# Pooled attention and a gated convolution FFN: v's first pooling addition by the loading DMA, ffn_in of sequence 0 by channel blocks, and a new order

## The chip, the cores and the metric

The kernel runs on one core of one Trainium2 chip. The metric is the device time in microseconds (us). TensorE (PE) multiplies matrices into PSUM; PEld is its weight load. VectorE (DVE), ScalarE (ACT) and GpSimd (POOL) work elementwise; SyncE (SP) issues DMAs only. All DMAs run on the same 16 DMA engines. Each engine works through its own instructions in program order and waits on semaphores for the others.

## The reference, cut to what matters

```python
def _attn_ref(q, k, v):                      # 8 sequences, 8 heads, 576 x 64, fp32
    k_p = k.reshape(B, H, Sp, 8, D).mean(axis=3)       # Sp = 72
    v_p = v.reshape(B, H, Sp, 8, D).mean(axis=3)
    scores = np.matmul(q, k_p.transpose(0, 1, 3, 2)) / np.sqrt(D)
    attn = softmax(scores)
    return np.matmul(attn, v_p)

def _moe_ref(x, w_in, conv_w, w_out):        # x: 8 x 576 x 512, d_ff = 1024
    h = np.maximum(x @ w_in, 0.0)
    conv_out = ...                           # depthwise, 3 taps along the sequence
    gate = 1.0 / (1.0 + np.exp(-conv_out))
    return h * gate @ w_out
```

The inputs and the output are fp32; inside, the kernel works in bf16 with fp32 sums.

## The kernel before

The eight sequences stand in four groups of two (groups 0 to 3). For each sequence the kernel loads q, k and v with a cast to bf16 (POOL's queue), pools and turns k, turns q, pools v, and then works through tiles of 128 rows: scores, maximum, shift, exponential, turning of e, product with v, division, turning of x. Then comes the FFN of the sequence: ffn_in, ReLU, the convolution with its sigmoid (a tanh), the gate, ffn_out and the store.

v's pooling is a tree of additions on VectorE. `load_v` (L280) brings a sequence with its eight neighbours side by side in 512 elements of a partition, in two DMAs of together 576 rows. `prep_v` (L459) adds the upper half to the lower three times (256, 128 and 64 elements wide, L464) and spreads the result over masked columns (L468). The ring of v has three buffers, so the load of sequence b waits until sequence b-3 is pooled.

`ffn_in` (L702) takes a block of 128 channels over half a sequence: four matmuls of 288 columns, and a ReLU for each block (`ffn_relu`, L713). Sequence 0 alone uses `ffn_in_tile` (L721) instead, a row tile of 128 (the last 64) against all eight channel blocks, with a ReLU for each tile (L736); it can begin with any one tile of x.

The convolution of a block runs either on TensorE with diagonal matrices (`ffn_conv`, L851) or, for the half sequences in `TAPS`, as three taps on ScalarE and VectorE (`ffn_tap`, L830, on a 576-wide view; L835, L837, L842). In group 2 and group 3, e and x are turned by DMAs on SP's queue (`att_send` L641, `att_out` L682), and in group 3 q as well (`q_send`, L505, one DMA transpose for a sequence). Outputs go through `osb`, a ring of five buffers, and are stored from SP's queue, in the last group from ScalarE's too.

Nothing is decided at run time. `Graph.ORDER` is a written-out list that a planner made: it names the operations in the order in which they are emitted, and an odd entry takes the second of two allowed engines (for a copy out of PSUM, VectorE first, ScalarE second). So it fixes the order on every engine and queue, POOL's loads and SP's transposes included. `FORMS` picks the TensorE tiling of some operations and `PLACES` the buffers and PSUM banks. The costs and the times of landing in `add(...)` served the planner alone and are not read at run time. A -1 in `ORDER` is a matmul on zeros (`fill`, L376) that keeps TensorE running while the first loads come in.

Of the kernel before, what the change touches and what calls it, by code (L numbers as in the profile page):

```python
# [33 lines left out]
class Graph:  # L34
# [25 lines left out]
    TAPS = ((4, 1), (5, 0), (5, 1), (6, 0), (6, 1), (7, 0))  # L60
    V_POOL = ()
    K_POOL = ()
    SHIFT_DVE = 1
# [3 lines left out]
        8, 26, 6, 2, -1, 18, 24, -1, 4, -1, -1, 36, -1, -1, 14, 38, -1, 10, 16, -1,  # L67
        -1, 34, 20, 22, 28, -1, 12, -1, -1, -1, 32, 30, 40, 92, 56, 94, 98, 96, 58, 104,
        101, 108, 103, -1, 106, 64, -1, 110, 42, 282, 48, 302, 284, 116, 50, 304, 112, 286, 114, 306,
        288, 118, -1, 308, 322, 324, 342, 310, 290, 120, 60, 313, 326, 328, -1, 344, -1, 362, 122, 346,  # L70
        364, 330, 348, 124, 366, 126, 333, 184, 293, 186, 334, 368, 62, 191, 294, 336, 189, 314, 68, 296,
        350, 52, 196, 353, 316, 192, 199, 354, 194, 370, 338, 356, 373, 504, 484, 74, 341, 506, 374, 486,
        0, 508, 318, 376, 510, 488, 358, 321, 524, 360, 216, 490, 526, 220, 218, 528, 378, 530, 222, 512,
        444, 380, 464, 394, 446, 66, 466, 448, 396, 514, 450, 54, 468, 400, 470, 128, 70, 298, 406, 301,
        44, 402, 398, 130, 382, 404, 132, 134, 472, 384, 46, 388, 386, 408, 475, 390, 410, 200, 532, 392,
        516, 492, 534, 434, 518, 495, 536, 202, 436, 438, 476, 538, 428, 478, 496, 430, 204, 228, 432, 498,
        231, 418, 440, 420, 412, 422, 442, 452, 416, 206, 414, 480, 72, 454, 224, 213, 424, 215, -1, 211,
        88, 209, 227, 252, 76, 426, 716, 483, 916, 255, 718, 544, 918, 520, 500, 720, 552, 503, 920, 523,
        696, 554, 136, 922, 698, 722, 456, 546, 557, 458, 540, 700, 876, 549, 248, 543, 878, 896, 560, 702,
        138, 251, 880, 704, 898, 724, 707, 460, 936, 140, 463, 562, 900, 727, 938, 582, 565, 142, 656, 584,  # L80
        902, 940, 80, 576, 882, 144, 594, 942, 578, 658, 586, 596, 580, 146, 708, 660, 598, 944, 884, 710,
        947, 624, 887, 148, 728, 150, 628, 588, 730, 626, 86, 712, 590, 715, 232, 948, 592, 924, 84, 904,
        736, 950, 78, 907, 606, 927, 738, 732, 888, 735, 608, 740, 612, 610, 890, 928, 742, 614, 930, 908,
        616, 744, 910, 952, 747, 630, 234, 748, 634, 954, 236, 632, 618, 750, 662, 932, 912, 620, 935, 152,
        752, 238, 622, 914, 754, 892, 243, 82, 646, 245, 894, 247, 636, 988, 241, 648, 1084, 990, 650, 1086,
        994, 992, 1100, 1088, 996, 1102, 600, 998, 1000, 154, 1116, 1104, 602, 1002, 1118, 604, 1030, 1106, 1120, 664,
        1032, 1004, 156, 568, 158, 1034, 160, 1122, 90, 676, 640, 1090, 638, 570, 642, 1092, 644, 678, 1006, 573,
        162, 558, 1012, 667, 680, 1008, 1014, 164, 1010, 652, 280, 1024, 1016, 668, 682, 1026, 670, 256, 1028, 260,
        566, 258, 1042, 263, 654, 1018, 1108, 1044, 1068, 1020, 1046, 1070, 772, 1022, 166, 672, 1072, 1052, 675, 168,
        1132, 684, 1054, 278, 1134, 774, 1056, 1136, 1058, 777, 264, 1138, 1322, 780, 1060, 1324, 1062, 1094, 687, 782,  # L90
        1124, 1096, 688, 1326, 785, 788, 550, 690, 1036, 266, 1306, 756, 1040, 268, 1328, 1308, 692, 1038, 790, 1064,
        695, 1110, 1074, 826, 1112, 793, 1076, 758, 1310, 820, 761, 1066, 828, 1126, 1098, 830, 832, 1128, 1312, 822,
        814, 1048, 824, 834, 1130, 816, 836, 860, 170, 818, 1140, 1050, 1338, 802, 862, 864, 808, 1330, 1340, 804,
        1342, 810, 806, 786, 1078, 172, 812, 274, 174, 270, 1080, 277, 1142, 1114, 273, 796, 1144, 850, 1082, 176,
        1570, 798, 854, 1572, 1146, 852, 838, 178, 800, 1574, 1332, 778, 840, 1344, 1334, 844, 842, 180, 1346, 1538,
        1230, 848, 1540, 846, 1232, 1542, 574, 866, 1234, 856, 1290, 1314, 1224, 868, 870, 1292, 1218, 1226, 872, 1220,
        1228, 1212, 1222, 1316, 1294, 1214, 1318, 1296, 1188, 1348, 1216, 874, 1298, 1190, 1544, 1238, 764, 1350, 1336, 1248,
        1206, 766, 858, 1192, 1546, 1240, 1300, 1208, 1250, 1164, 1320, 1210, 1302, 1576, 1554, 1506, 1252, 1304, 1166, 1264,
        1556, 769, 1200, 1254, 1508, 1352, 980, 1169, 1558, 1256, 1202, 794, 1510, 1194, 1560, 1242, 1410, 1204, 1578, 1196,
        182, 1412, 1258, 1422, 1414, 1562, 1266, 982, 1198, 1244, 1522, 1236, 1794, 1424, 1524, 1246, 1796, 1172, 1426, 1526,  # L100
        1512, 1548, 1798, 1174, 985, 1528, 1550, 1274, 1177, 1268, 1552, 1746, 1428, 1276, 1748, 1278, 1416, 1170, 1750, 1430,
        1564, 1260, 1432, 1580, 762, 1270, 1566, 1418, 1262, 1582, 1280, 770, 1752, 1272, 1420, 1398, 1282, 1530, 1436, 1404,
        1284, 1386, 1496, 972, 1568, 1286, 1472, 1406, 1388, 986, 1408, 1474, 974, 1498, 1514, 1392, 977, 1288, 956, 1488,
        964, 1390, 1476, 1394, 1490, 1532, 1396, 1400, 1534, 966, 1402, 1500, 1536, 1478, 1516, 1434, 1778, 1502, 1518, 1762,
        958, 1480, 1764, 1520, 1148, 1454, 1780, 1800, 1492, 1378, 1584, 969, 1482, 1150, 1494, 1802, 1766, 961, 1380, 1484,
        1768, 1626, 1178, 1153, 1456, 1644, 1462, 1628, 1782, 1154, 1646, 1458, 1630, 1638, 1648, 1464, 1804, 970, 1460, 1156,
        1806, 1383, 1640, 978, 1486, 1466, 1632, 1438, 1180, 1504, 1770, 1642, 1634, 1446, 1662, 1754, 1182, 1784, 1448, 1636,
        1664, 1440, 1468, 1808, 1656, 1674, 1772, 1185, 1450, 1158, 1666, 962, 1774, 1702, 1668, 1442, 1658, 1161, 1786, 1756,
        1704, 1444, 1670, 1452, 1758, 1362, 1660, 1706, 1370, 1760, 1672, 1470, 1708, 1650, 1372, 1776, 1694, 1686, 1788, 1652,
        1384, 1696, 1364, 1654, 1790, 1375, 1610, 1676, 1678, 1698, 1792, 1854, 1367, 1688, 1612, 1700, 1162, 1690, 1848, 1728,  # L110
        1586, 1680, 1692, 1376, 1856, 1730, 1615, 1842, 1712, 1682, 1368, 1602, 1858, 1732, 1850, 1684, 1186, 1714, 1860, 1734,
        1604, 1736, 1716, 1616, 1844, 1720, 1738, 1862, 1852, 1588, 1722, 1864, 1740, 1618, 1846, 1607, 1724, 1890, 1884, 1718,
        1608, 1872, 1710, 1726, 1886, 1742, 1594, 1894, 1620, 1744, 1591, 1596, 1910, 1592, 1888, 1874, 1599, 1878, 1896, 1918,
        1866, 1912, 1880, 1876, 1868, 1882, 1898, 1810, 1870, 1914, 1818, 1900, 1892, 1920, 1916, 1834, 1902, 1922, 1934, 1904,
        1924, 1820, 1938, 1906, 1936, 1812, 1908, 1928, 1623, 1926, 1624, 1354, 1932, 1930, 1826, 1600, 1823, 1940, 1836, 1825,
        1828, 1942, 1356, 1814, 1968, 1358, 1817, 1960, 1360, 1838, 1831, 1952, 1841, 1832, 1944, 1970, 1946, 1973, 1954, 1975,
        1948, 1962, 1957, 1951, 1976, 1958, 1964, 1967, 1978, 1984, 1982, 1981, 1986, 1990, 1989,
    )
    FORMS = (
        0, 1, 0, 0, 1, 1, 1, 1, 1, 0, 0, 0, 0, 1, 0, 0, 0, 0, 0, 0, 0, 0, 1, 1, 1, 0, 0, 0, 0, 0, 0, 1, 1, 1, 0, 1, 1, 1, 1, 1,  # L120
    )
    PLACES = (
        0, 1, 2, 1, 2, 1, 2, 0, 1, 2, 1, 0, 2, 3, 2, 3, 0, 1, 0, 2, 1, 3, 0, 1, 4, 2, 5, 2, 0, 0, 4, 1, 1, 0, 0, 1, 1, 6, 0, 0,
        2, 2, 2, 1, 3, 4, 0, 5, 1, 1, 6, 0, 4, 0, 0, 4, 1, 4, 2, 0, 6, 1, 2, 0, 0, 4, 1, 0, 0, 2, 3, 1, 2, 0, 6, 1, 2, 4, 2, 3,
        0, 1, 1, 0, 4, 1, 5, 6, 0, 0, 0, 0, 2, 2, 0, 0, 0, 1, 1, 4, 1, 1, 2, 2, 1, 0, 6, 7, 2, 2, 0, 2, 4, 1, 3, 0, 0, 2, 2, 0,
        2, 0, 6, 4, 6, 1, 0, 0, 2, 0, 1, 6, 1, 1, 2, 2, 4, 0, 0, 2, 0, 2, 6, 3, 0, 2, 4, 1, 0, 0, 6, 0, 2, 2, 4, 1, 0, 6, 2, 0,
        4, 3, 0, 6, 2, 2, 3, 1, 0, 1, 1, 4, 0, 4, 6, 1, 5, 1, 2, 2, 3, 0, 0, 1, 1, 4, 0, 0, 0, 6, 1, 0, 0, 3, 2, 0, 1, 1, 1, 6,
# [45 lines left out]
def kernel(  # L173
# [83 lines left out]
    def shift_by_dve(g, t):  # L257
        return g >= Graph.SHIFT_DVE

# [611 lines left out]
    def ffn_tanh(b, fb, ps):  # L871
        g, i = where[b]
        if fb % 2:
            t = buf("tg", b, fb // 4)[:, fb // 2 % 2]
        else:
            t = buf("gT", g)[:, fb, i * S:(i + 1) * S]
# [484 lines left out]
```

## Time and profile before

| what | value |
|---|---|
| runs (us) | 220.47, 220.76, 222.03; median 220.76 |
| profiled execution | 220.57 us, its span 218.9 us |
| mean granted TensorE clock | 0.987 |
| instructions in the span | 6761 |
| DMA | 32.63 MB, mean 149 GB/s |
| L464, v's additions on VectorE | 24 in 12.9 us |
| L726, ffn_in of sequence 0 by tiles | 160 matmuls in 8.9 us |
| L705, ffn_in by blocks | 448 matmuls in 65.1 us |

The span is the profiled execution from its first to its last instruction; the device time is a little longer. A group of instructions is written as its line, engine, operation and tile, the count, the busy time and mean of one in ns, and then the idle time of its engine just before it with what ended it. PE is shown as busy while a matmul is in flight, and matmuls overlap.

### The profile page before, as it was taken

To read this page: it belongs to the slowest core of one execution; us is meant where nothing else is said; L and a number is where in the kernel's file an instruction comes from. 1 tells how busy PE (TensorE), PEld (TensorE's weight loads), DVE (VectorE), ACT (ScalarE), POOL (GpSimd) and SP (SyncE) were. 2 spreads that over 40 slices of the span, in tenths; PEclk is the share of its full clock that TensorE was granted. 3 is DMA by queue.
4 is the path that set the end of the run, shared out by engine and by line. 5 is a ranking of instruction groups with operands and counts; after the bars stand their busy time and mean duration, and the time that the engine had idled before them with its cause. 6 is when DMAs were issued, how large, how long until landed. Compare 5 with 4: busy or idle time off the path is not lost.

```text
span 218.9 us, 6761 instructions
## 1 busy us (share of the span) xinstructions
PE 203.1 (93%) x2839; PEld 139.5 (64%) x2839; DVE 193.6 (88%) x338; ACT 158.8 (73%) x267; POOL 41.7 (19%) x65
## 2 busy tenths in 40 slices
PE   6797999978999999999999799999999999999991
PEld 2556799765588886766777576566556556564450
DVE  5768976999999999998999889999999999997821
ACT  2046738797998869976787659788699889998120
POOL 7943322032025002000000030203200220520000
PEclk9799999999999999999999999999999999999997
DMA  5999999999999998999567745457457657421685
GB/s 83 166 177 203 207 206 208 207 207 206 208 206 159 188 167 135 154 198 140 98 134 108 125 94 88 88 119 121 89 118 175 140 120 182 112 48 24 160 219 175
DMA packets 48834, 32.63 MB, mean 149 GB/s; under 512 B 28300, under 2 KB 44324, under 8 KB 48804
## 3 DMA queue, kind: packets, MB, share of 16 engines
q0 software_dynamic: 16288, 16.26, 46.7%
q1 hardware_dynamic: 31396, 14.24, 34.2%
q10 hardware_dynamic: 1120, 1.70, 2.6%
q8 instruction: 22, 0.36, 0.7%
q14 instruction: 8, 0.07, 0.1%
HBM read 32.52 MB, written 9.44 MB: 192 GB/s over the span
## 4 chain that ended last, share of the span: by engine, by line
PE 58%; DMA 20%; DVE 11%; POOL 4%; issue 3%; ACT 1%; POOLq 0%; DVEq 0%; ACTq 0%
PE psum L906 24%; PE psum L705 20%; DMA qp<-in_q_dram 18%; PE psum L862 6%; PE psum L660 4%; DVE negm L586 3%; DMA eT<-e 3%; DVE sd L598 2%; DVE v L464 2%; DVE x L675 1%; POOL kk L265 1%; PE psum L635 1%; POOL qp L265 1%; PE psum L560 1%; PE psum L692 1%
## 5 line engine op out<-in xcount | busy, mean ns | idle before, releaser
L906 PE MATMUL psum<-w_out_sb,gT 128*128 128x512 bf16 (+1 forms) x296 | 69.8, 373 | 0.7 <-DVE gT L898 0.6
L705 PE MATMUL psum<-xT,w_in_sb 128*128 128x288 bf16 x448 | 65.1, 286 | 0.2
L705 PEld LDWEIGHTS <-w_in_sb 128*128 128x128 bf16 x448 | 41.5, 98 | 15.9 <-issue 1.4
L906 PEld LDWEIGHTS <-gT 128*128 128x128 bf16 x296 | 27.6, 98 | 25.9 <-issue 0.8
L714 ACT ACTIVATE hT<-psum 128x576 bf16<-128x576 f32 x56 | 35.2, 647 | 10.9 <-PE psum L705 10.5
L837 DVE SCALAR_TENSOR_TENSOR tg<-hT,convw,tg 128x576 f32<-128x576 bf16 x48 | 37.5, 824 | 0.2
L586 DVE TENSOR_REDUCE negm<-psum 128x8 f32<-128x576 f32 (+2 forms) x37 | 27.2, 750 | 1.6 <-PE psum L573 1.1
L675 DVE TENSOR_TENSOR x<-psum,r 128x512 bf16<-128x512 f32 (+1 forms) x37 | 25.6, 691 | 1.3
L917 ACT COPY osb<-psum 128x512 f32<-128x512 f32 x30 | 17.4, 582 | 10.8 <-DVE osb L917 4.2
L789 POOL COPY hT<-hT 128x252 bf16<-128x252 bf16 x8 | 6.2, 780 | 98.0 <-ACT hT L714 89.7
L862 PE MATMUL psum<-hT,dw 64*64 64x288 bf16 (+2 forms) x608 | 19.7, 261 | 1.5 <-DVE x L675 0.5
L660 PE MATMUL psum<-vm,eT 128*128 128x65 bf16 (+5 forms) x240 | 19.0, 222 | 2.0 <-DMA eT<-e 1.9
L598 DVE TENSOR_TENSOR sd<-psum,negm 128x576 f32<-128x576 f32 x27 | 20.0, 751 | 0.3
L862 PEld LDWEIGHTS <-dw 64*64 64x64 bf16 x608 | 15.3, 107 | 6.7 <-issue 5.2
L660 PEld LDWEIGHTS <-eT 128*128 128x128 bf16 (+1 forms) x240 | 15.1, 100 | 6.5 <-DMA eT<-e 2.5
L624 ACT ACTIVATE e<-sd 128x576 bf16<-128x576 f32 x27 | 18.0, 680 | 0.8 <-DVE sd L598 0.6
L835 ACT ACTIVATE tg<-hT,convw 128x576 f32<-128x576 bf16 x24 | 18.2, 775 | 0.1
L842 ACT ACTIVATE gT<-tg 128x576 bf16<-128x576 f32 x24 | 15.8, 683 | 1.6 <-DVE tg L837 1.6
L877 ACT ACTIVATE tg<-psum 128x576 bf16<-128x576 f32 x20 | 12.9, 649 | 3.8 <-PE psum L862 3.8
L877 ACT ACTIVATE gT<-psum 128x576 bf16<-128x576 f32 x20 | 13.0, 649 | 3.3 <-PE psum L862 3.0
L464 DVE TENSOR_TENSOR v<-v 128x1280 bf16<-128x1280 bf16 (+2 forms) x24 | 12.9, 538 | 1.9 <-DMA v<-in_v_dram 1.8
L898 DVE TENSOR_TENSOR gT<-gT,hT 128x2304 bf16<-128x2304 bf16 x10 | 13.5, 1352 | 0.1
(83 smaller groups left out, 250.8 us busy)
## 6 DMA issues: line engine op xcount, KB each, us to landing
out_dram<-osb SPq DMA_DIRECT2D x58, 128.0 KB, 2.4
v<-in_v_dram POOLq DMA_DIRECT2D x8, 512.0 KB, 12.5
qp<-in_q_dram POOLq DMA_DIRECT2D x7, 576.0 KB, 14.4
kk<-in_k_dram POOLq DMA_DIRECT2D x3, 1152.0 KB, 13.3
out_dram<-osb ACTq DMA_DIRECT2D x12, 128.0 KB, 2.7
w_in_sb<-in_moe_w_in_dram POOLq DMA_DIRECT2D x2, 512.0 KB, 17.1
w_out_sb<-in_moe_w_out_dram POOLq DMA_DIRECT2D x1, 1024.0 KB, 24.1
kk<-in_k_dram POOLq DMA_DIRECT2D x2, 288.0 KB, 5.1
```

The costliest lines, as they stand in the source:

```text
L586: nc.vector.tensor_reduce(out=a["m"][0:rows], in_=a["s"][0:rows, :, 0:2 * KW].rearrange("p a (h s) -> p a h s", s=Sp), axis=AX.X, op=OP.ma ...
L598: nc.vector.tensor_tensor(out=a["d"][0:rows], in0=a["s"][0:rows, :, 0:2 * KW].rearrange("p a (h s) -> p a h s", s=Sp), in1=a["m"][0:rows]. ...
L624: nc.scalar.activation(out=dst, in_=src, func=ACT.Exp, scale=1.0 / (POOL * 8.0),)
L660: nc.tensor.matmul(out=a["o"][lo:hi, h // 4, (h % 4) * (D + 1):(h % 4 + x1 - x0) * (D + 1)], lhsT=a["eT"][:, j, lo:hi], rhs=buf("vm", b)[: ...
L675: nc.vector.tensor_tensor(out=a["x"][0:rows].rearrange("p (a h d) -> p a h d", a=2, d=D), in0=ov[:, :, :, 0:D], in1=r[0:rows].unsqueeze(3) ...
L705: nc.tensor.matmul(out=banks(ps)[:, j, 0:SC], lhsT=w_in_block(dc, fb), rhs=buf("xT", g)[:, dc, i * S + j * SC:i * S + (j + 1) * SC], start ...
L714: nc.scalar.activation(out=h_of(b)[:, fb].rearrange("p (a s) -> p a s", a=2), in_=banks(ps)[:, :, 0:SC], func=ACT.Relu, scale=0.5,)
L835: nc.scalar.activation(out=acc, in_=h, func=ACT.Identity, scale=w)
L837: nc.vector.scalar_tensor_tensor(out=acc, in0=h, scalar=w, in1=acc, op0=OP.mult, op1=OP.add)
L862: nc.tensor.matmul(out=banks(pss[r ^ c])[c * D:(c + 1) * D, j, lo:hi], lhsT=dw[r * D:(r + 1) * D, tap * n_fb + fb, :], rhs=hT[r * D:(r + 1 ...
L877: nc.scalar.activation(out=t.rearrange("p (a s) -> p a s", a=2), in_=banks(ps)[:, :, 0:SC], func=ACT.Tanh, scale=0.5,)
L906: nc.tensor.matmul(out=bank(ps)[0:rows, columns], lhsT=buf("gT", g)[:, fb, t * P:t * P + rows], rhs=w_out_sb[:, fb, columns], start=(fb == 0),
```

## The change

1. `V_SUM = (4, 5, 6, 7)`: the v of these sequences is loaded in two halves of 256 elements a row, and the second half is added to the first by the DMA. `prep_v` leaves out its first addition for them. The second half waits for the first to land, on POOL's queue.
2. `BY_TILE = ()`: sequence 0 takes `ffn_in` by channel blocks like the others.
3. The results of the last group go to buffers `late`, eight halves of the four qp buffers, instead of `osb`.
4. `ffn_tap` and `ffn_tap_tanh` see the same elements as two runs of 288; tap 1 waits for the ReLU of its block alone and no more for the wrapped ends.
5. New lists `ORDER`, `FORMS` and `PLACES`. On POOL's queue the two parts of q of sequence 0 and the pooling matrix now stand ahead of the head mask and the identity; the first half of v4 stands ahead of the keys of group 2; q of sequence 4 stands ahead of w_out; between the halves of v4 stand the keys of group 2 and q7, between those of v5 q6 and q5, between those of v6 the keys of group 3. The two DMA transposes of q on SP's queue, which stood around the load of v7 on either side, follow the second half of v7. One store of group 0 goes out early. On VectorE stand two copies of kT less, two of qT less, one of xT less, one of kT (`copy_keys`) more and one of the output more; ScalarE has the reverse. 19 `fill` matmuls stay.

The options `ACC`, `WRAPS`, `CROSS` stand at values that leave the code as it was. The changed costs are the planner's. The diff, cut:

```diff
+    ACC = 2
+    V_SUM = (4, 5, 6, 7)
+    WRAPS = 4
+    CROSS = ()
+    BY_TILE = ()
...
-            "hT": 2, "gT": 2, "xT": 2, "qT": 3, "kk": 1, "qp": 4, ..., "s": 2}
+            "hT": 2, "gT": 2, "xT": 2, "qT": 3, "kk": 1, "qp": 4, ..., "s": 2, "late": 8}
...
+    half_qp = [t.rearrange("p h s -> p (h s)")[:, i * 1024:(i + 1) * 1024] for t in buffers["qp"] for i in range(2)]
+    buffers["late"] = [t.bitcast(FP32) for t in half_qp]
...
-    def load_v(b):
+    def load_v(b, half=0):
         rows = v[b].rearrange("h (sp r) d -> (h sp) (r d)", r=POOL)
         vt = buf("v", b)
-        nc.gpsimd.dma_start(
-            out=vt[:, 0:4, :], in_=rows[0:4 * P].rearrange("(j p) x -> p j x", p=P)
-        )
-        nc.gpsimd.dma_start(out=vt[0:TB, 4, :], in_=rows[4 * P:])
+        n = POOL * D // 2 if b in Graph.V_SUM else POOL * D
+        lo, how = half * n, dict(accum_op=OP.add) if half else {}
+        nc.gpsimd.dma_start(out=vt[:, 0:4, 0:n], in_=rows[0:4 * P, lo:lo + n].rearrange("(j p) x -> p j x", p=P), **how)
+        nc.gpsimd.dma_start(out=vt[0:TB, 4, 0:n], in_=rows[4 * P:, lo:lo + n], **how)
...
     def ffn_copy(g, t, ps, copy, columns=slice(0, d_model)):
-        osb = buf("osb", g, t)
+        osb = buf("late" if g == 3 else "osb", g, t)
...
+        if twice:
+            lv[b] = add({"POOL": 1.33}, key, lambda: load_v(b, 1), uses=[vtok[b]], after=[lv[b]], land=(LATE, kb / 2, RATE))
...
         for step, d in enumerate((0.81, 0.49, 0.32, 0.65)):
+            if step == 0 and b in Graph.V_SUM:
+                continue
...
-        if b == 0:
+        if b in Graph.BY_TILE:
             for t in range(5):
```

## The prediction

> **What bounds the kernel now.** I read the busy shares first, then the same in stretches of 10 us, then what TensorE waits for, the chain that ended last, the groups of instructions, and the DMA landings. The profiled execution took 220.57 us, its span is 218.9, so 1.7 us lie around it; the median of the three runs shown is 220.76, 0.19 more. The sum below is made against 220.57 and 0.19 is added at its end. A measurement of this kernel can tell about 1% (2.2 us) from no change.
>
> The page's busy line:
>
> ```profile
> PE 203.1 (93%) x2839; PEld 139.5 (64%) x2839; DVE 193.6 (88%) x338; ACT 158.8 (73%) x267; POOL 41.7 (19%) x65
> ```
>
> Two engines are nearly full. The stretches (first PE, PEld, DVE, ACT, POOL busy, then granted clock and DMA share) show where they are not:
>
> ```profile
> 10.00:20.00 10.00, 8.25 (x179) 6.08 (x176) 7.45 (x15) 4.86 (x10) 3.69 (x6) 0.91 1.18 185
> 30.00:40.00 10.00, 9.88 (x198) 9.54 (x199) 6.86 (x15) 7.39 (x10) 1.79 (x3) 1.00 1.23 206
> 40.00:50.00 10.00, 8.71 (x222) 6.88 (x215) 9.74 (x19) 8.55 (x16) 2.86 (x4) 1.00 1.23 208
> 60.00:70.00 10.00, 10.00 (x139) 8.34 (x138) 9.83 (x18) 9.37 (x18) 4.13 (x6) 1.00 1.16 187
> 120.00:130.00 10.00, 8.37 (x107) 6.00 (x105) 8.47 (x16) 7.24 (x12) 1.65 (x2) 1.00 0.65 112
> 200.00:210.00 10.00, 10.00 (x68) 4.72 (x67) 6.64 (x9) 3.13 (x7) 0.00 (x0) 1.00 0.61 157
> ```
>
> Up to about 50 us loads set the pace: the DMA share is above 1 and TensorE idles 7.0 us in all (43.0 busy of 50). From 50 to 210 TensorE idles only 4.1 us of 160, and VectorE from 40 to 200 only 5.7 of 160. What TensorE waits for between 50 and 214 us:
>
> ```profile
> PE psum L660 <- DMA eT<-e: 1.9, 2, 1.5
> PE psum L906 <- DVE gT L898: 0.6, 1, 0.6
> PE psum L862 <- DVE x L675: 0.5, 2, 0.3
> ```
>
> So TensorE is the bound there, with VectorE close behind: taking VectorE work away can return no more than the waits that VectorE causes. The chain that ended last passes through these pieces (start, duration, what):
>
> ```profile
> 24.84 24.12 DMA qp<-in_q_dram
> 49.01 0.69 PE psum L494 x18
> ...
> 74.87 0.81 DVE v L464
> ...
> 83.93 0.82 DVE v L464
> ```
>
> The first two say that TensorE, in program order, stood at sequence 4's q transposes until that load landed at 49.0. The other two are first additions of v's pooling, which the change removes.
>
> **Part by part.** The rows that price it:
>
> ```profile
> L464 DVE TENSOR_TENSOR v<-v 128x1280 bf16<-128x1280 bf16 (+2 forms) x24 | 12.9, 538 | 1.9 <-DMA v<-in_v_dram 1.8
> L726 PE MATMUL psum<-xT,w_in_sb 128*128 128x128 bf16 (+1 forms) x160 | 8.9, 214 | 0.0
> L705 PE MATMUL psum<-xT,w_in_sb 128*128 128x288 bf16 x448 | 65.1, 286 | 0.2
> L736 ACT ACTIVATE hT<-psum 128x1024 bf16<-128x1024 f32 (+1 forms) x5 | 4.6, 945 | 1.1 <-PE psum L726 1.0
> ```
>
> *Channel blocks for sequence 0.* 160 matmuls in 8.9 us go; 64 of 288 columns come. Dense runs of L705 on the chain are four in 0.49 us, so 64 cost 7.84: 1.06 less. They lie at 29 to 38 us, where TensorE is 9.88 full, so this is on the path. ScalarE's ReLU goes from 5 x 0.945 to 8 x 0.647 = +0.45 us, beside TensorE (ScalarE 7.4 of 10 there). But fb 1 comes only after two of the four convolutions, and blocks need three x tiles before the first matmul where one was enough. Bounds 0 and -1.06; I take **-0.8**, near the row.
>
> *Order of the loads.* On POOL's queue the q load of sequence 4 now stands ahead of w_out. w_out is 2.1 MB of the fp32 source; the landings of q3 (41.0), w_out (46.1) and q4 (49.0) put its share at 5 us, so q4 lands near 44 and the 0.92 us wait at 49.0 goes. w_out then lands near 49, against its first use at 50.9. Behind the wait stands a 0.6 us wait for VectorE's gate (L898, above), so part of it returns. Bounds 0 and -0.92; I take **-0.5**. At the start, the pooling matrix comes ahead of the head mask and the identity (POOL 2.86 to 3.56 and 4.45 to 4.98, 1.2 us), which the first real matmul at 7.84 waits for. But ffn_in at 29.2 still waits for w_in (landing 28 to 30). Bounds 0 and -1.2; I take **-0.2**.
>
> *v's first addition.* VectorE loses 4 x 0.815 = 3.26 us, at 74.87, 83.93, 94.11 and 115.44. By the new list's choice of engine VectorE also loses two kT copies, two qT copies and one xT copy (0.60 + 0.87 + 0.39, all before 35 us, where it idles 9.7 of 40) and gains one kT copy and one output copy (0.65 + 0.61); in the full stretch the net is -2.0. ScalarE takes the reverse, beside 27% idle. TensorE's waits that VectorE causes, between 50 and 214, sum to 1.3 by the waits; the starts of consecutive matmuls put all stalls there at some 6.5 us, about 3.5 of them at VectorE's rows. Bounds 0 and -3.26; I take **-1.3**, the waits' row.
>
> *The accumulating loads.* Each of four v loads becomes two. Queue 0's packet records show 98 ns for a row of 1024 bytes and 60 ns for one of 512. A v has 576 rows, 36 per DMA engine: 3.5 us before, 36 x (60 + 60) = 4.3 if an addition costs a copy. No trace here shows an accumulating packet. Lower bound the copy, 2.2 us per half; upper bound the bytes it touches twice over, 120 ns, 4.3 us; I take 3.2. The second half waits on POOL for the first to land; behind it stand the next loads, and behind those VectorE. Following the list with the old landings (v3 54.5, q7 63.3): v4's sum lands about 68 to 70 and is first read about 74; v5's about 80 to 82, read about 86; pair 3's keys about 92, read 96; v6's 94, read 99; v7's 100, read 114. The cover is 4 us at the tightest, so **0**. The second issues cost POOL 4 x 1.33 us (0.76 + 0.56 each) where it has no other work until the first wrap at 127.6. A missed cover stalls VectorE one for one.
>
> The Trainium skill, Collectives: The Full Stack (The bandwidth ceiling: the fold count and why AG ≠ RS ≠ AR), says that an add inside the DMA is slow because it needs two source reads per chunk and so doubles the read-side traffic. No run here shows it; by that rule a half would take the 4.3 us of the upper bound, v4 would land near 70, and the sum would not move, but the cover at v5 would fall to 4 us.
>
> *Transposes of q.* They move behind the last v issue:
>
> ```profile
> 88.39 5.33 SPq L506 DMA_TRANSPOSE qT<-qp  x1
> ...
> 97.13 4.03 SPq L506 DMA_TRANSPOSE qT<-qp  x1
> ```
>
> The first, issued while v7 was in flight (84.3 to 92.2), held SP 1.3 us longer than the second. SP's queue carries the e transposes that TensorE waits for (1.9 us at 124 and 170), but these are 25 us later; bounds -1.9 and +1.3 (the same collision met by an e transpose that now goes ahead of them); I take **0**.
>
> *Later output buffers.* The last group's results go to the space of q. Output copies waited 6.9 us on stores, all after 203, beside TensorE's closing run (13.1 us of L906 without a gap): **0**. Dropping the wait of tap 1 on the wrap, likewise 0: ScalarE is not the bound. The rewritten tap views have the same elements: 0. Each of the 19 fill matmuls stays.
>
> *The new list itself* can open or close waits anywhere: bounds -1.5 and +1.5, about what the old one's largest TensorE gap (1.5 at 124) is worth; 0.
>
> **Sum:** -0.8 - 0.5 - 0.2 - 1.3 = -2.8; 220.57 - 2.8 = 217.8, and with 0.19 **218.0**.
>
> **Rivals.** *All of it arrives*: -1.06, -0.92, -0.2 and -2.6 (the waits' row doubled, as the matmul starts suggest) give -4.8, 216.0. For it speaks that VectorE has 98% in the middle; against, that TensorE's own work after 50 us is unchanged. *Hidden*: TensorE is so dense that only the blocks' 0.8 remains: 220.0. For it, TensorE 10.0 of 10 at 60 to 90 and 160 to 210; against, that two removed additions are on the chain. *The accumulate is dear*: slower. If one costs more than about 6 us on the DMA engines (170 ns a packet, near three copies), v5's sum passes its first read; at 9 us each is 6.8 above a copy, and behind one another on POOL's queue pair 3 and v6 land some 15 us late against 4 of cover: +11, so about 229. For it: a DMA share of 1.0 to 1.3 until 100 us. Against: the cover of 4 to 14 us. *A new in-order wait*: an e transpose on SP meeting the accumulates, two stalls as long as the one at 124, and no gain: 220.8 + 3 = 223.8. The change not doing what it says has nothing for it: the first additions are skipped by the code.
>
> **Chances.** Forecast 0.40 (own range 216.8 to 219.2, two thirds of it under 218.55, the 1% line), all arrives 0.24, hidden 0.20, dear accumulate 0.10, new wait 0.06. Faster 0.26 + 0.24 = 0.50, same 0.14 + 0.20 = 0.34, slower 0.16. The range 215.0 to 223.0 leaves out the two slow cases and a little under the fast one.
>
> **What would show it.** Right: 20 first, second and third additions of v instead of 24, VectorE near 190; 512 matmuls of 288 columns and none by tiles; no wait at q4's transposes; v5's next addition not waiting for DMA. Wrong: "DVE v <- DMA v" of several us near 75 to 100, POOL standing long at second v issues, e transposes taking over 4 us; TensorE idle over 5 us between 50 and 210.

## The result and the profile after

The changed kernel takes 226.14 us (median of 224.96, 225.81, 226.47, 226.58) where the kernel before takes 220.75: ratio 1.0244, 95% interval 1.0202 to 1.0286. It is 2.4% slower; 218.0 was forecast, with 223.0 as the upper end. The profiled execution took 224.96 us, its span is 223.3. For two of the experiments below only the time is told, since their profiled execution was a disturbed one.

The page's busy line, and the two groups that answer to those of the prediction (of the 24 instructions of v's three additions 20 are left, and sequence 0's ffn_in is now in L713):

```profile
PE 203.5 (91%) x2737; PEld 137.9 (62%) x2737; DVE 191.4 (86%) x331; ACT 160.9 (72%) x273; POOL 48.0 (21%) x73
```

```profile
L472 DVE TENSOR_TENSOR v<-v 128x640 bf16<-128x640 bf16 (+2 forms) x20 | 9.7, 485 | 0.2
L713 PE MATMUL psum<-xT,w_in_sb 128*128 128x288 bf16 x512 | 72.9, 288 | 3.3 <-DMA xT<-x 2.2
```

Everything that was to be removed is removed. ffn_in fell from 65.1 + 8.9 = 74.0 to 72.9, VectorE from 193.6 to 191.4. Up to 97 us the changed kernel is ahead by about as much as was forecast: VectorE's shifts of the scores (L598 before, L606 after), each second one compared with its counterpart, start 2.7 to 3.7 us earlier up to the fifteenth (97 us), and the 25th ffn_out matmul 2.5 us earlier (80 us). The whole lead is there from the first shift on (2.9 us at 49 us), before the first of the removed additions would have run. Then the lead is lost: the 49th ffn_out matmul is 0.8 us late (101 us), the 73rd 5.4 (136 us), and the last one 4.0. From 2.9 us ahead to 4.0 behind, 6.9 us are lost. The stretches say where (columns as in the prediction; the first line is the kernel before, whose other two stretches stand in the prediction, the next three are the changed one):

```profile
90.00:100.00 10.00, 9.27 (x177) 6.47 (x177) 9.27 (x14) 7.87 (x13) 0.00 (x0) 1.00 1.28 168
```

```profile
40.00:50.00 10.00, 8.46 (x227) 6.09 (x227) 9.81 (x18) 9.46 (x16) 2.67 (x3) 1.00 1.24 208
90.00:100.00 10.00, 7.93 (x127) 5.01 (x125) 6.09 (x9) 5.79 (x10) 2.22 (x2) 0.83 1.20 167
120.00:130.00 10.00, 8.07 (x126) 5.82 (x117) 6.61 (x13) 5.70 (x10) 0.00 (x0) 0.83 0.43 76
```

Between 40 and 50 us, where the wait for q4 was to go, TensorE's busy time hardly changes (8.46, before 8.71). In the stretches from 90 and from 120 us TensorE idles about 2 us, VectorE idles too, and the granted clock is 0.83: both engines that were full stand still. (In what follows, a stand is a time in which TensorE does nothing.) The clock's record has two stretches at half clock, each 3.41 us long, from 95.8 and from 123.1 us; the kernel before has none between 12 and 216 us. The chain shows what comes ahead of each:

```profile
93.25 0.28 PE psum L643 x5
93.53 0.15 PE psum L568 x3
93.68 2.07 issue
95.75 0.40 PE psum L568 x13
```

```profile
111.64 4.82 DMA xT<-x
...
119.40 3.79 DMA xT<-x
```

The first stand, 2.07 us in the midst of 16 equal matmuls, waits for nothing that the profile shows ("issue"). The DMA records have a queue of the kind "instruction":

```profile
q8 instruction: 21, 0.34, 0.7%
```

These are 21 pieces of 16 KB, one for about 130 of TensorE's 2737 matmuls with their weight loads; a piece takes 0.9 to 1.0 us when nothing is beside it. One starts at 93.4 and takes 1.07 us, and TensorE goes on 1.3 us after its landing. It is the same 1.3 us after the landing of a piece in three more of the profiles below (after_again, e1, e9). So TensorE seems to have run out of instructions; this is read from the order in time. How much TensorE had done since the last piece doesn't explain it alone: 190 weight loads ran between this piece and the one before it (85.3), but in the kernel before 209 ran between the pieces at 85.0 and 94.8, and no stand followed.

The second stand (1.93 us at 121.3) is a wait for x to be turned by DMA; these transposes took 3.8 and 4.8 us from issue to release where the page's median landing is 2.5. What POOL and SP did around the first stand (start, duration, what; in brackets the wait before it):

```profile
82.22 0.79 POOL L293 DMA_DIRECT2D v<-in_v_dram  x1 [1.41 <-DVE vm L476]
...
93.82 1.34 POOL L293 DMA_DIRECT2D v<-in_v_dram  x1 [10.27 <-DMA v<-in_v_dram]
```

```profile
87.30 7.73 SPq L514 DMA_TRANSPOSE qT<-qp  x1
...
103.64 3.30 SPq L514 DMA_TRANSPOSE qT<-qp  x1
```

The first half of v7 took 10 us to land, and only then did its second half go out. The last byte of v lands at 99.7 us instead of 92.3, and between 84 and 93 v's loads share the DMA engines with group 2's first two transposes of e (issued at 79.9 and 81.5, landed at 90.4 and 92.0) and with that of sequence 6's q. By the packet records, in steps of 2 us, loads move 134 to 208 KB a microsecond from 60 to 82 us and 23 to 88 between 84 and 92, though the DMA share there is 1.44 and so higher.

Two stands (4.0 us) and half of two stretches (3.4 us) are 7.4 us, less the 1.5 us stand that the kernel before has at 124: by this estimate 5.9 of the 6.9 us lost.

### The profile page after: what moved, and what is told of

Read it like the earlier page. It is cut to its first block, busy times and chain, and to the rows that moved or that the text cites. A ratio compares the mean times of both kernels' runs of the same rounds, so it can differ in the third digit from the quotient of the medians.

```text
span 223.3 us, 6566 instructions
## 1 busy us (share of the span) xinstructions
PE 203.5 (91%) x2737; PEld 137.9 (62%) x2737; DVE 191.4 (86%) x331; ACT 160.9 (72%) x273; POOL 48.0 (21%) x73
## 3 DMA queue, kind: packets, MB, share of 16 engines
q10 hardware_dynamic: 880, 1.25, 2.1%
## 4 chain that ended last, share of the span: by engine, by line
DVE 44%; PE 31%; DMA 10%; issue 9%; ACT 2%; SPq 1%; POOL 1%; DVEq 0%; POOLq 0%
PE psum L929 13%; PE psum L713 9%; DVE tg L850 8%; DVE negm L594 7%; DVE x L683 6%; DMA xT<-x 5%; DVE sd L606 4%; PE psum L875 3%; DMA qp<-in_q_dram 3%; DVE gT L921 3%; DVE gT L913 3%; DVE kk L425 2%; DVE r L681 2%; DVE gT L862 2%; PE psum L668 2%
## 5 line engine op out<-in xcount | busy, mean ns | idle before, releaser
L713 PE MATMUL psum<-xT,w_in_sb 128*128 128x288 bf16 x512 | 72.9, 288 | 3.3 <-DMA xT<-x 2.2
L713 PEld LDWEIGHTS <-w_in_sb 128*128 128x128 bf16 x512 | 48.1, 98 | 19.5 <-DMA xT<-x 3.1
L722 ACT ACTIVATE hT<-psum 128x576 bf16<-128x576 f32 x64 | 40.0, 648 | 16.8 <-PE psum L713 16.5
L797 POOL COPY hT<-hT 128x252 bf16<-128x252 bf16 x8 | 5.1, 632 | 93.4 <-ACT hT L722 81.8
L293 POOL DMA_DIRECT2D v<-in_v_dram x12 | 12.3, 1027 | 40.3 <-DMA v<-in_v_dram 28.0
L875 PE MATMUL psum<-hT,dw 64*64 64x288 bf16 (+2 forms) x608 | 20.2, 274 | 0.3 <-ACT hT L722 0.3
L606 DVE TENSOR_TENSOR sd<-psum,negm 128x576 f32<-128x576 f32 x27 | 20.0, 753 | 0.5
L668 PE MATMUL psum<-vm,eT 128*128 128x130 bf16 (+5 forms) x240 | 19.2, 222 | 0.9 <-DMA eT<-e 0.8
L875 PEld LDWEIGHTS <-dw 64*64 64x64 bf16 x608 | 15.8, 113 | 4.8 <-issue 3.6
L940 ACT COPY osb<-psum 128x512 f32<-128x512 f32 x24 | 13.9, 585 | 3.4 <-PE psum L929 3.1
```

Of the source, the lines that this page charges most:

```text
L606: nc.vector.tensor_tensor(out=a["d"][0:rows], in0=a["s"][0:rows, :, 0:2 * KW].rearrange("p a (h s) -> p a h s", s=Sp), in1=a["m"][0:rows]. ...
L668: nc.tensor.matmul(out=a["o"][lo:hi, h // 4, (h % 4) * (D + 1):(h % 4 + x1 - x0) * (D + 1)], lhsT=a["eT"][:, j, lo:hi], rhs=buf("vm", b)[: ...
L713: nc.tensor.matmul(out=banks(ps)[:, j, 0:SC], lhsT=w_in_block(dc, fb), rhs=buf("xT", g)[:, dc, i * S + j * SC:i * S + (j + 1) * SC], start ...
L722: nc.scalar.activation(out=h_of(b)[:, fb].rearrange("p (a s) -> p a s", a=2), in_=banks(ps)[:, :, 0:SC], func=ACT.Relu, scale=0.5,)
L875: nc.tensor.matmul(out=banks(pss[r ^ c])[c * D:(c + 1) * D, j, lo:hi], lhsT=dw[r * D:(r + 1) * D, tap * n_fb + fb, :], rhs=hT[r * D:(r + 1 ...
```

## The experiments

The theories of the loss:

- T1: the place of the two q transposes.
- T2: adding in flight loads the DMA engines.
- T3: dense small matmuls eat instructions faster than they come.
- T4: the new order by itself.
- T1', which came after the first runs: each second half waits for its first to land, and these waits stretch v's loads into group 2's transposes.
- T5, which came last: where in TensorE's stream an instruction fetch (one of the 16 KB pieces) falls.

The table has each run's ratio to the kernel before on the same chip, and from its profile the end of v's last data packet, TensorE's stands over 0.95 us from 80 to 130 us, and the half-clock stretches between 12 and 212 us.

| run | ratio (95%) | v landed, us | stands, us (at) | half clock |
|---|---|---|---|---|
| before | 1 | 92.3 | 1.48 (124) | 0 |
| after | 1.0244 (1.0202 to 1.0286) | 99.7 | 2.07 (94), 1.93 (121) | 2 |
| after_again | 1.0238 (1.0131 to 1.0346) | 100.7 | 2.89 (94), 2.39 (122) | 2 |
| e1_plain_over | 1.0190 (1.0084 to 1.0296) | 99.7 | 2.62 (95), 2.38 (121) | 1 |
| e2a_q6_early | 1.0185 (1.0071 to 1.0298) | 106.4 | 1.02 (88), 0.97 (95), 1.81 (115) | 1 |
| e2b_q_both | 1.0274 (1.0119 to 1.0430) | | | |
| e5_q5_half | 1.0105 (1.0019 to 1.0191) | 99.7 | 2.36 (94) | 0 |
| e9_q_left_out | 1.0058 (1.0011 to 1.0105) | 100.2 | 1.22 (88), 1.52 (95), 1.66 (120) | 0 |
| e10_few_loads | 0.9957 (0.9916 to 0.9997) | 93.7 | 2.38 (118) | 1 |
| e8_dve_adds | 1.0044 (1.0001 to 1.0088) | 96.7 | 1.27 (89), 1.25 (96) | 0 |
| e3_vsum_old_order | 1.0529 (1.0417 to 1.0640) | 115.2 | 8.97 (88), 2.53 (116) | 4 |
| c1_acc45 | 0.9934 (0.9891 to 0.9977) | 96.4 | 0.97 (95) | 0 |
| c2_acc45_half | 0.9881 (0.9792 to 0.9969) | 92.8 | none | 0 |
| c4_whole | 0.9959 (0.9910 to 1.0009) | | | |
| d1_v7_upper | 1.0109 (1.0029 to 1.0188) | 93.7 | 2.53 (118) | 1 |
| d2_v7_upper_half | 0.9912 (0.9873 to 0.9952) | 92.8 | none | 0 |
| d3_acc456_half | 1.0115 (1.0018 to 1.0211) | 97.5 | none | 0 |
| d4_q4_half | 0.9910 (0.9867 to 0.9953) | 94.2 | none | 0 |
| d5_q3_back | 1.0069 (1.0019 to 1.0119) | 93.5 | 2.13 (120) | 0 |

**Is it the addition in flight (T2)?**

```diff
-        lo, how = half * n, dict(accum_op=OP.add) if half else {}
+        lo, how = half * n, {}
```

> The second half of v of sequences 4 to 7 is written plainly over the first instead of being added to it (the sum with the upper half is left out); same waits, bytes, order. T2 (accumulating packets load the DMA engines so that the q transposes beside them become long and stall TensorE): the transposes of q of sequence 6 falls from 7.7 to about 5 us, the 2.07-us stand of TensorE at 93.7 us goes, with its half-clock stretch, and the time falls to 219 to 222. T1 (the place of the two q transposes on SP) and T3 (instruction fetch) and T4 (the new order): addition in flight is nearly free (packets 59 ns at the median), so 225 to 227 as after, with both stalls of 1.9 to 2.1 us and both half-clock stretches still there.

Both stands stay, and the time is, within the intervals, where it was. The packets say that adding is not free, but cheap: of 512 bytes, a plain one takes 60 ns and an adding one 82 to 84 (the 59 ns of the expectation is that of a plain one), so a half costs 36 x 84 = 3.0 us of each engine. T2 falls.

**Is it the place of q's transposes (T1)?** In the first run `q_send` of sequence 6 is moved in `ORDER` to before the first `att_send` of group 2; in the second that of sequence 7 also goes to where sequence 6's was.

> Only the transposing DMA of q of sequence 6 is moved: from behind v's last load to before group 2's first transpose of e, where SP is idle and nothing of group 2 is queued behind it. T1: the stand of TensorE at 93.7 us and its 3.4 us at half clock go, so 2.1 + 1.7 = 3.8 us, and the time is 222 to 223; the later stall at 121 us stays if it belongs to sequence 7's transpose, or goes too (218 to 219) if it was only the lateness handed on. T3 (instruction fetch starved by dense small matmuls): the stand stays though the transpose is away, 225 to 227. T4: no change, 225 to 227.

> Both transposing DMAs of q are moved forward: sequence 6's as in the run before, sequence 7's to where sequence 6's was (right behind the scores that free its buffer), out of the middle of group 2's transposes. T1: the stall on the xT transpose at 121 us goes as well as that at 93.7, 7.4 us together at most, and the time is 218 to 220. If the transpose of sequence 7 now sits beside v's last loads as that of sequence 6 did, the first stall stays: 221 to 223. T3 and T4: 225 to 227.

Earlier, the transposes meet other loads: with sequence 6's moved, v now lands at 106.4, two short stands of 1.02 and 0.97 are there in place of the 2.07, and in both runs the loss is, within the intervals, the same. A place among the loads is no cure. Next, all but one block of the two transposes is left out:

```diff
-            out=buf("qT", b).rearrange("p (n x) -> p n x", x=P), in_=buf("qp", b).rearrange("p h s -> p (h s)")
+            out=buf("qT", b)[:, 0:P], in_=buf("qp", b).rearrange("p h s -> p (h s)")[:, 0:P]
```

> The transposing DMAs of q of sequences 6 and 7 move one block of 128 columns instead of the whole tile (the rest of q of these two is left out); all else as after. T1 (the q transposes beside v's loads are what starves TensorE): the stand in the scores at 93.7 us goes and the time is 219 to 222. T1' (v's loads, which now end at 100 us instead of 93 because each second half waits for the first one's landing, meet group 2's transposes of e, and it is these two that delay the instruction fetch): a stand of 1 to 3 us near 88 to 95 us is still there, 223 to 226.

The time lies between the two expectations: most of the loss goes (1.0058), yet there are stands at 88, 95 and 120 us, each too short for the half clock. So q's transposes have a part in it, but they are not needed for a stand.

**Is it the number of instructions (T3)?** `FORMS` of `prep_q` of sequence 5, both halves: 64x64 tiles become 128x64.

> Only q of sequence 5 is turned by TensorE with half as many matmuls (36 for each half instead of 72), so fewer instructions in the microseconds ahead of 93.7 us. T3: fewer instructions are fetched, the stand of 2.07 us and its half-clock stretch go, and the time is 222 to 223. T1: the fetch is late because of what the DMA engines do, the stand stays or shifts, 225 to 227. A cost of its own: the form may make the scores that use it longer or shorter by some tenths of a microsecond.

The records show half of what the expectation says: sequence 5 has 72 matmuls here, not 144, and the lighter form 36, so 36 matmuls and their 36 weight loads go. The stand at 94 stays (2.36 us), so T3 fails as put, and that the time falls to the 222 us that T3 named is luck. It fell because the stand at 121 and both half-clock stretches were gone (the stand of 2.36 falls into two of the clock's stretches, see the end). No theory expected this; T5 below answers it.

**Is it the late end of v's loads (T1') or the order (T4)?**

```diff
+        if not (half and b >= 6):
+            nc.gpsimd.dma_start(out=vt[:, 0:4, 0:n], ...
```

> The adding loads of the second half of v of sequences 6 and 7 are cut to their last 64 partitions (32 KB of 288 KB each; the rest of these sums is left out); both q transposes, the order and all waits stay. T1: the q transpose of sequence 6 still runs beside v7's first load, the stand at 93.7 us stays, 224 to 227. T1': the loads end at about 93 us, little lies beside the transposes, the fetch is on time and the stand goes: 218 to 222.

The stand at 94 is gone, with q's transposes and the order as they were. The same stretch in after and in this run, DMA share and GB/s last:

```profile
92.00:96.00 4.00, 1.93 (x44) 1.14 (x37) 2.37 (x3) 2.59 (x5) 2.18 (x2) 0.98 1.34 165
```

```profile
92.00:96.00 4.00, 3.26 (x63) 2.05 (x62) 3.59 (x5) 3.07 (x7) 0.00 (x0) 1.00 0.36 15
```

TensorE works 3.26 of 4 us instead of 1.93 where the loads are almost done. Next, no sum by DMA, both halves side by side, VectorE adding again, all in the new order:

```diff
-        lo, how = half * n, dict(accum_op=OP.add) if half else {}
+        lo, how = half * n, {}
+        at = slice(lo, lo + n)                # out=vt[:, 0:4, at], ...
...
+        if step == 1 and b in Graph.V_SUM:
+            prep_v(b, 0)
```

> The change without its pooling by DMA: both halves of v of sequences 4 to 7 are loaded plainly side by side (the second no longer waits for the first one's landing) and VectorE makes the four first additions again, in the new order. VectorE gets 4 x 0.81 = 3.3 us more. T1': the loads end earlier, the stand at 93.7 us and what follows go, and the time is 219 to 222 in spite of VectorE. T1 and T4 (the new order and the q transposes' place are the loss): the stand stays and VectorE's additions come on top, 226 to 230.

The ratio is 2% better than that of after although VectorE does 3.3 us more: the sums by DMA lose more than they save, and what is left of T4 is at most 0.9%. The other way round, the sums alone in the order of before:

```diff
+        twice = b >= 4
+        for half in range(1 + twice):         # the second with accum_op
...
+        if step == 0 and b >= 4:
+            return
```

> The kernel before with one part of the change alone: v of sequences 4 to 7 is added up by the loading DMA (both halves issued one behind the other where the one load was) and VectorE's four first additions are gone; order, q transposes and blocks as before. T4 (the new order and the place of the q transposes cost, the sum by DMA itself gains): 218.5 to 220.5, the 1.3 us of the forecast's term or less. T1' in its wide form (any load that waits for another's landing runs into the transposes): POOL stands about 10 us at each landing, the loads end near 100 us, a stand of 1 to 3 us appears near 90 to 100 us, 221 to 225.

Worse than either theory said. The waits of this run:

```profile
POOL v L287 <- DMA v<-in_v_dram: 47.9, 5, 20.7
...
PE psum L502 <- DMA qp<-in_q_dram: 9.0, 1, 9.0
```

POOL stands 47.9 us for v's loads to land, with loads of q queued behind, and TensorE waits 9.0 us for one of these. So waits for a landing do cost, but most of it by another path than T1' names: not by a collision with transposes, but by the loads behind them in the queue. And the new order of the loads, far from being the loss (T4), is what made the sums bearable. Then four runs on one chip: after once more, sums for 4 and 5 only (its edit below), the same with the lighter form of q of sequence 5, and no sums at all.

```diff
+        summed = b in (4, 5)                  # 6 and 7: whole rows in one go, VectorE adds
```

> The changed kernel itself once more, beside the three below on the same chip: 225 to 227, with a stand of about 2 us of TensorE in the scores near 94 us that fills over half of one of the clock's 3.41-us stretches, and the next stretch at half clock.

> The change, but only v of sequences 4 and 5 is added by the loading DMA; v of 6 and 7 is loaded whole in one go where its first half was, and VectorE makes these two first additions (2 x 0.81 = 1.6 us more of it). T1' (landing waits stretch v's loads into group 2's transposes): the loads end near 95 us instead of 99.7, no stand near 94 us is over 1.7 us, no half-clock stretch there, and the time is 219 to 222. T4 (the new order): 223 to 227, the stand stays. T1 (q's transposes): also 223 to 226, since they stay where they are.

> The run before with q of sequence 5 turned by half as many matmuls. T1' with T3 (fewer instructions make a late fetch cheaper): 217.5 to 220.5, faster than before the change, with no stand over 1.5 us near 94 us. If the instruction count hardly matters: as the run before, 219 to 222.

> No addition by DMA at all: v of sequences 4 to 7 is loaded whole in one go where the first half was, VectorE makes all four first additions (3.3 us of it), in the new order. T1': loads end by 95 us, no half-clock stretch, 219.5 to 222: what is left of the new order without the pooling by DMA. If the loads' end is not what matters, it is as the run with both halves plain side by side, 221.

After stands at 1.0238 and the version with two sums at 0.9934: the late two sums cost 3.0%, about 6.7 us. With the lighter form of q on top it is 0.9881, faster than the kernel before. With none by DMA it is 0.9959: the two early sums are worth little, if anything.

**Which wait is it?** v of sequence 7 goes to an unused half buffer, and its first half goes out 11 us earlier; all four sums stay. The second run has the lighter form of q of sequence 5 on top, the third sums sequences 4, 5 and 6 by DMA.

```diff
+    def v_of(b):
+        return buffers["v"][2][:, :, POOL * D // 2:] if b == 7 else buf("v", b)
```

> The whole change with all four sums by DMA and the same order, but v of sequence 7 goes to the upper half of the buffer whose lower half holds sequence 5, which nothing else uses by then; its first half is therefore issued right behind sequence 6's first half (near 72 us instead of 82), and each adding half finds its first half landed. T1' in its narrow form (what costs is that the last landing wait stretches the loads to 100 us, not the addition): the loads end near 94 us, the stand near 94 us falls under 1.7 us or goes, and the time is 218.5 to 222. If adding in flight itself is dear beside the transposes, or the new order is: 224 to 227 as after.

> The run before with q of sequence 5 turned by half as many matmuls. T1': 217.5 to 220.5, at or below the version with two sums by DMA (219.4), since VectorE does 1.6 us less. If the adding loads are dear in themselves: 222 to 224, as the change with this form of q alone.

> The version with sums by DMA for sequences 4 and 5 and the lighter form of q, with sequence 6 summed by DMA too: only sequence 7 is loaded whole. It tells which of the two late sums costs. Sequence 7's landing wait (10.3 us, the longest) alone: 218.5 to 220 as with two sums or a little less. Sequence 6's too: 221 to 223, with a stand of over 1 us near 94 us again.

As T1' said, v lands at 93.7 and the stand near 94 is gone: taking the long wait of v7's second half away takes this stand away. In the first run the stand at 118 stays with its half clock, so it gains only half (1.0109). The lighter form of q alone took the other half (e5, 1.0105). With both it is 0.9912, with all four sums in place: each stand has its own cure, and by and large the cures add up. The third run, with sequence 6 summed and not 7, came out at 1.0115 from few runs, while its profile has no stand; it stays open whether sequence 6's wait alone costs.

By what path v7's wait delays the fetch stays open too, and T1' has it wrong in part. In after the stand begins at 93.7 us and v7's second half is issued only at 93.8 (in after_again 93.3 and 94.1). So the loads behind it, up to 100 us, can't have made this fetch late; only what ran before can, v6's second half, v7's first and the transposes. Nor does the end of the loads measure the stand (e2a: 106.4 us, stands of 1.02 and 0.97), nor how much runs beside the transposes: between 84 and 92 us d1 loads 83 KB a microsecond where after loads 60, and its q transpose holds SP for 8.54 us instead of 7.73.

**Why does the form of q, 30 us earlier, matter (T5)?** It takes 72 instructions (36 matmuls, 36 weight loads) out of TensorE's stream, and so moves every later fetch. The fourth run takes 72 out at another place (`FORMS` of `prep_q` of sequence 4, both halves), the fifth puts 72 back (sequence 3, on top of the second run). In the records sequence 4's run at 47 to 51 us and sequence 3's at 41 to 46, not at the 65 and 60 us, and by 72, not the 144, of the expectations; for what T5 says it is the same.

> The run with v of sequence 7 in the other buffer, with q of sequence 4 (near 65 us) turned by half as many matmuls instead of q of sequence 5 (near 88 us): 144 instructions of TensorE fewer ahead of 117 us, as in the version with sequence 5's, but the dense ones near 88 us stay. T5 (an instruction fetch that falls into a transpose of x holds it up, and the stand at 118 us hangs on where in TensorE's stream the fetch falls): the fetch moves by the same 144 instructions, the transposes of x that are waited for near 118 us land within 3 us, the stand of 2.8 us and its half-clock stretch go, 218 to 220. T3 (dense matmuls near 88 us): the stand stays, 221.5 to 224.5.

> The version with v of sequence 7 in the other buffer and the lighter form of q of sequence 5, with q of sequence 3 (near 60 us) turned by twice as many matmuls: the 144 instructions are put back ahead of 117 us, so that the fetches fall where they fell before the lighter form. T5: the stand near 118 us comes back, 221 to 224. T3: it stays away, 218 to 220.

Both came out as T5 said (in the fifth the stand comes back with 2.13 us, but falls into two of the clock's stretches, and no half clock follows). The last transpose of x ahead of the place where TensorE stood, from the chains of d1, d2, d4 and d5 in this order:

```profile
116.06 4.41 DMA xT<-x
```

```profile
116.86 2.43 DMA xT<-x
```

```profile
117.38 2.42 DMA xT<-x
```

```profile
118.02 3.99 DMA xT<-x
```

Instruction pieces start at 117.4, 119.2, 120.3 and 119.2: inside the transpose in the first and last, at or behind its end in the two between. The other records agree. In the 17 profiles of the table, 101 transposes of e and x behind 102 us have a piece starting within 2 us of their issue: 95 of them take 3 us or more to land, 3.9 at the median. 312 have none from 2 us ahead of their issue to their landing: 306 of them take less than 3 us, 2.55 at the median. And 81 times between 60 and 210 us three or more packets, most of them of transposes, stood over 1.2 us and ended together; 75 of these ends lie 1.5 to 2.8 us after a piece started, a stretch that holds an eighth of the time.

## Why the prediction was wrong, step by step

- *TensorE is the bound, with VectorE close behind*: right, and the reason that stands of TensorE count in full. But the sum asked only what would be taken away from a full engine.
- *Channel blocks, -0.8*: L713 holds 1.1 us less than both rows before, and ffn_in starts at 27.9 instead of 29.2. *q4 ahead of w_out, -0.5*: TensorE has no wait for a load left at 44 to 56 us. These two and the start (-0.2) were reckoned at 1.5 us; the lead at 49 us is 2.9. A part of it may be the half-clock stretch that the profile before has at 8 to 12 us (1.7 us).
- *v's additions, -1.3*: **no run shows this gain.** The lead is 2.9 us at 49 us, before the first removed addition (74.9 us in the kernel before), and still 2.9 at 97 us, when three of the four are behind it. Where nothing stands, four sums by DMA (d2, 0.9912) gain no more than two (c2, 0.9881). That the lead equals the 2.8 of the sum is luck: the early terms gave more and this one nothing that can be seen. Three of the four versions in whose profile nothing stands gain 0.9 to 1.2%, 1.9 to 2.6 us (the fourth, d3, doesn't), but all have the lighter form of q, whose own price is not known.
- *The accumulating loads, 0*: **this step failed.** On one chip the late two sums cost 3.0%, about 6.7 us. The numbers that the step looked at held: 3.2 us a half was taken, 3.0 came, v7's sum was to land at 100 and its last byte landed at 99.7. The Trainium skill (Collectives: The Full Stack, The bandwidth ceiling: the fold count and why AG ≠ RS ≠ AR) has an add in the DMA double the reads; here the packet takes 1.4 times a copy's, so a doubling of its time is not seen. And VectorE never waited for v. But the step compared the landings with VectorE's reads alone, v7's with its read at 114. It gave no price to what else is on the DMA engines meanwhile: group 2's transposes and TensorE's own instructions. Of POOL's wait it said that the next loads stand behind it; behind the longest, 10.3 us, stood v7's own second half. Taking that wait away (d1) takes the stand at 94 away; how the wait makes the fetch late stays open, as said above.
- *Transposes of q, 0, bounds -1.9 and +1.3*: **the bound was mis-sized.** The transpose met by loads took 7.73 us instead of 5.33, but its price was not SP's time: with the two transposes cut to a block each, the loss falls from 2.4 to 0.6%. Nor is it the transpose alone, since in d1 it takes 8.54 us and no stand follows near 94.
- *The new list, 0, bounds of 1.5*: the stand at 121 cost 1.93 and 1.7. The bound was the largest stand of before, and that one, 1.5 us, was too short to halve the clock. Whether a fetch falls into a transpose that TensorE waits for is an accident of the list: 72 instructions fewer ahead of it were enough to undo it.
- *Rivals*: POOL standing long at second issues was named as a sign of being wrong and came (28.0 us in all), but the price that dear accumulate put on it did not (VectorE waiting, 229). The new in-order wait had the right number of stands, two, by chance: it named an e transpose that meets the accumulates, not a fetch, and had no price for the clock. Of the other signs, TensorE idled 7.7 us between 50 and 210 instead of 4.1; that an e transpose takes over 4 us was no good sign, as one took 8.2 in the kernel before.

## What to carry to other kernels

When a load is split so that one part waits for another, ask what else the transfers run into once they are moved, not only whether their reader is still in time. Count TensorE's instruction fetch among the users of the DMA engines: here it met both loads and transposes. A stand of TensorE of 2 us that falls into one of the clock's stretches cost 3.7 us here, one of 1.5 us only itself: price stands near 1.8 us as a step, and look at the granted clock before comparing two orders. And when a forecast's total comes out, check that its parts did.

## What the runs showed of the hardware

- **Half clock.** In the 17 profiles of the table, cut by the clock record's own grid of 3.41 us, all 10 stretches between 12 and 212 us in which TensorE idled 1.9 us or more were followed by one at half clock, none of 964 with less than 1.8, and two of the three between. The Trainium skill (TensorE: Matmul & The Clock Gate, What's actually happening) gives this free-running window and lets an idle one throttle; here a bit over half of it idle was enough. The grid is not tied to the kernel: the stand of 2.62 us in e1 fell into two windows and no half clock followed, the one of 2.07 in after fell into one.
- **Instruction fetch.** TensorE's comes in pieces of 16 KB on the DMA engines. The Trainium skill (Runtime: NRT & Kernel Launch, Instruction fetch mechanics) calls its cost mostly hidden; in four profiles (after, after_again, e1, e5) TensorE stood 2.07 to 2.89 us beside loads and transposes, and went on 1.3 to 1.5 us after a piece had landed.
- **Fetch and transpose.** A transpose of e or x took 3.9 us to land at the median when a piece started within 2 us of its issue (101), and 2.55 when none was near (312).
- **DMA.** With transposes and stores beside them, v's loads fell from 134 to 208 KB a microsecond (60 to 82 us of after) to 23 to 88 (84 to 92 us). An adding packet of 512 bytes took 82 to 84 ns, a plain one 60.
